# Row products of two token chunks with seven block products for eight, columns first, sums by DMA

## The chip, the cores and the metric

The kernel runs on one core of a Trainium2 chip. The metric is device time in microseconds of one launch, taken as the median of several runs. A core has five engines with instruction queues of their own: PE (TensorE, matmuls; PEld is its weight load), DVE (VectorE), ACT (ScalarE), POOL (GpSimd) and SP, which here only issues DMA transfers. They meet through semaphores.

## The reference

The input is attention data q, k, v of 2 batches, 8 heads, 768 positions, head size 64, and five weight matrices. Three steps follow one another:

- block attention: every query sees the keys closer than 16 positions and 24 block summaries (maximum of 32 keys, mean of 32 values), with a softmax over both;
- layer 1 on the 1536 tokens x 512: `g = x @ w_gate`, `val = x @ w_val`, then `(silu(g) * val) @ w_out`, with 1536 hidden columns;
- layer 2: `h = x @ w_in` with 2048 hidden columns, a piecewise square (0 below -1, h above 1, `(h + 1)^2 / 4` between), then `@ w_out` to the 1536 x 512 result.

All arrays are fp32.

## The kernel before

**Tiling.** The 1536 tokens are three chunks of 512 (`CH`). Every fp32 matmul operand is cut in two parts, `hi` (rounded to fp32r) and `lo` (the rest), and one product is three matmuls: hi*hi, hi*lo, lo*hi (`PASSES`, `mm3` L985, matmul at L987). Hi comes from a copy on ACT or DVE (`copy` L383), lo from a subtraction (`subtract` L924, instruction at L926), nearly always on DVE. A product with a layer's first weights is called a column product, one with its `w_out` a row product.

**Chunk 0** is done first, beside the attention of all chunks (`step_jobs`, `use_jobs` L1096). Its weights are decoded there, kept in DRAM (`keep_pack` L911) and read again later.

**Chunks 1 and 2 are done jointly** (`JOINT`, in the trace from about 266 us). Their column products already use a scheme with seven block products in the place of eight (`FORMS`, `form` L1306, `quad_jobs` L1325): two halves of the inner dimension, two blocks of hidden columns and the two chunks make a 2 x 2 by 2 x 2 block product. It needs sums of weight blocks (`add_group` L1208, cut in `group_hi`, `group_lo`), sums of input blocks (`add_term` L1269, cut in `term_hi`, `term_lo`), and joins of the results (`fork` L1318, `join` L1322). Layer 1 has 12 such quads, layer 2 has 8; each is seven forms of six matmuls of 512 columns.

Their row products are plain. `row_jobs` (L1374) issues, per chunk and per 128 hidden columns f, four row products of 128 outputs or 128 tokens (`row_product` L1005) into four accumulators in PSUM; `row_feed` (L1364) reads the kept weights and cuts them once per chunk, and `split_hidden` (L1171) cuts each hidden tile once. The rows of chunk 1 stand between the columns; those of chunk 2 follow. Each layer ends with copies out of PSUM (`y_out` L1405, or `put_jobs` L1085 with a store).

**Order.** Every piece of work is a job with its engines and durations, a rank, what it needs and which buffers it takes. `Plan.emit` (L127) is a list scheduler: it picks again and again the ready job with the least modelled start plus `URGE * rank`, chooses the engine that ends first by the modelled cost, and emits it. So it fixes the order of instructions on each engine's queue, SP's too; at run time each engine takes its queue in that order and waits for semaphores. The ranks are built from the constants `T`.

Of the kernel before, what the change touches and what calls it, by code (L numbers as in the profile page):

```python
# [25 lines left out]
 'urge': 0.00016,  # L26
 'weight': (0.925, 772.894, 0.282, 0.289),
# [3 lines left out]
 'd': (-5637.212, 41085.045),  # L31
 'load': (3008.479, 4747.053),
 'high': (-2836.042, 3239.532),
 'bits': (-935.349, 1886.602),
 'keep': (-57947.518, -5594.531),
 'read': -11449.662,
 'hi': (-27701.488, 1102.421),
 'lo': (-11590.763, -2406.109),
 'head_rank': (5076.154, -7290.563, -60395.485, -15458.656),
 'half_rank': -29616.131,  # L40
 'start': 464.292,
 'unit': 1.932,
 'e0': 462.563,
 'a1': (62.363, 14.301),
 'a2': (116.213, 16.636),
 'x': (617.322, 3982.825),
 'j': (2797.217, 10463.422),
 'g': (1.248, 6.748),
 'q': (0.007, 0.113),
 'jr': (1234.441, 846.231),  # L50
 'jw': (1404.409, 766.537),
 'rw': 858.964,
 'js': (-6034.078, 1900.145),
 'gh': (746.555, 1544.378),
 'gl': -1712.874,
 't': 484.136,
 'th': 822.2,
 'tl': -35.6,
 'qp': (-30.096, -19.417, -3.899, 35.81, 32.684, -24.767, -40.513),
 'qf': -562.767,  # L60
 'qj': -1653.995,
 'qa': 2416.954,
 'rs': 3036.454,
 'rh': 887.986,
 'x2': 255.064,
 'r2': (400.241, 30033.282),
 'first': (-5645.576, -144.845),
 'st_q': (-2034.21, 345.71),
 'st_qt': (-732.561, -1914.119),
 'st_sc': (-685.966, -444.589),  # L70
 'st_mx': (-35663.85, -1356.97),
 'st_ex': (-3778.03, 3307.182),
 'st_iv': (-5276.379, 81.698),
 'st_no': (742.266, -11947.766),
 'st_wt': (-4363.695, 165.258),
 'st_pt': (-52297.254, -1058.814),
 'st_av': (-394.819, -213.378),
 'st_xh': (133.16, 1680.548),
 'st_xl': (-10069.461, -3131.586),
 'kl': (-42181.744, 4874.082),  # L80
 'kp': (3666.397, -5596.737),
 'kt': (-3814.781, -1844.408),
 'km': (-77721.471, 514.179),
 'kc': (2433.202, -51674.2),
 'vl': (-198.108, 134.248),
 'vm': (2794.065, -1853.404),
 'vs': 26403.355,
 'vo': (-29543.71, -26442.98),
 've': (-15678.039, 5229.978),
 'ql': (-31980.946, -7672.979),  # L90
# [141 lines left out]
def tile_block_attention_ffn(  # L232
# [1141 lines left out]
    def row_jobs(c, st, fs, t):  # L1374
# [6 lines left out]
        for f in fs:  # L1381
            row_feed(c, st, f, t + UNIT * (f - fs[0]))
# [107 lines left out]
```

## Time and profile before

| what | value |
|---|---|
| runs | 613.59, 615.02, 615.07 us; median 615.02 us |
| span of the profiled execution | 612.5 us |
| PE / DVE / ACT / POOL busy | 98% / 82% / 57% / 4% |
| matmuls | 3737 |
| moved by DMA | 95.01 MB |

The profile gives the span of its execution, from the first instruction to the last, and no time of its own for what lies around it; the span is 2.5 us below the median. A busy PE is not a PE at its peak, since matmuls are pipelined; the chain of waits and the spacing of matmuls tell its pace. A line number is often that of a helper: L987 is every matmul with cut operands, L385 a copy on ACT, L389 a copy on DVE, L926 a subtraction; the names of output and inputs tell them apart (`acc_y` are row products; `qg`, `qv`, `qi` are column products of chunks 1 and 2; `pg`, `pv`, `pi` those of chunk 0).

### The profile page before, as it was taken

How to read it: one execution, taken by the hardware profiler on the slowest of the kernel's cores; microseconds unless marked ns; L12 is line 12 of the kernel's file. 1: busy time of each engine (PE TensorE's matmuls, PEld its weight loads, DVE VectorE, ACT ScalarE, POOL GpSimd, SP SyncE). 2: the span in 40 equal slices, each digit the busy share in tenths (PEclk: the TensorE clock that was granted, in tenths of full speed). 3: DMA queues.
4: the chain of work that ended last, by engine and by line, in shares of the span. 5: the costliest groups of instructions: out<-in, count | busy, mean ns of one | idle time of the engine just before them, and what ended most of it. 6: DMA issues, size and time to landing. Idle time of an engine off the chain costs nothing.

```text
span 612.5 us, 9841 instructions
## 1 busy us (share of the span) xinstructions
PE 600.7 (98%) x3737; PEld 498.4 (81%) x3737; DVE 502.4 (82%) x910; ACT 347.4 (57%) x634; POOL 26.8 (4%) x54
## 2 busy tenths in 40 slices
PE   8699999999999999999999999999999999999997
PEld 7589888778888888888888888888888888888886
DVE  4788999989899898887788877788888897886662
ACT  5787687877979576454443433322268554742112
POOL 3320201000000000000000000000000000000000
PEclk9979999999999999999999999999999999999999
DMA  8999996999896398132110211123300131103411
GB/s 228 291 303 279 328 303 251 327 266 317 315 339 206 138 307 309 71 139 68 70 68 1 103 70 68 35 104 102 138 20 16 34 138 35 36 0 116 160 35 69
DMA packets 79199, 95.01 MB, mean 155 GB/s; under 512 B 36272, under 2 KB 62128, under 8 KB 79152
## 3 DMA queue, kind: packets, MB, share of 16 engines
q1 hardware_dynamic: 79152, 94.39, 47.9%
q8 instruction: 29, 0.48, 0.3%
q14 instruction: 18, 0.15, 0.1%
HBM read 73.40 MB, written 20.97 MB: 154 GB/s over the span
## 4 chain that ended last, share of the span: by engine, by line
PE 96%; DMA 1%; SPq 1%; ACT 1%; POOL 0%; issue 0%; ACTq 0%; POOLq 0%
PE acc_y L987 38%; PE qi L987 12%; PE qv L987 9%; PE qg L987 9%; PE pi L987 7%; PE pv L987 6%; PE pg L987 6%; PE px L588 2%; PE sc L637 2%; PE pt L683 1%; DMA raw<-in_moe_w_val_dram 1%; PE pk L518 1%; SPq L442 1%; PE pq L569 1%; PE pk L296 1%; SPq L884 1%
## 5 line engine op out<-in xcount | busy, mean ns | idle before, releaser
L987 PE MATMUL acc_y<-dd,h 128*128 128x512 f32 (+1 forms) x387 | 88.4, 387 | 0.0
L987 PEld LDWEIGHTS acc_y<-dd,h 128*128 128x128 f32 x387 | 72.4, 188 | 14.9
L987 PE MATMUL acc_y<-h,dd 128*128 128x512 f32 x288 | 66.1, 389 | 0.0
L987 PEld LDWEIGHTS acc_y<-h,dd 128*128 128x128 f32 x288 | 54.1, 188 | 11.2
L385 ACT ACTIVATE dd<-wf 128x1024 fp32r<-128x1024 f32 x25 | 26.4, 1057 | 61.3 <-PE acc_y L987 61.3
L987 PE MATMUL qi<-xj,wjs 128*128 128x512 f32 x192 | 46.4, 389 | 0.0
L987 PE MATMUL acc_y<-wA,h 128*128 128x512 f32 x192 | 45.8, 389 | 0.0
L903 DVE SCALAR_TENSOR_TENSOR wb<-dd 128x1024 int32<-128x1024 int32 x34 | 41.6, 1227 | 2.3 <-ACT dd L385 1.4
L926 DVE TENSOR_TENSOR wA<-wb,wA 128x1024 fp32r<-128x1024 f32 x34 | 41.6, 1231 | 1.8 <-ACT wA L385 1.1
L987 PE MATMUL pi<-y,wA 128*128 128x512 f32 x128 | 42.4, 392 | 0.0
L987 PEld LDWEIGHTS qi<-xj,wjs 128*128 128x128 f32 x192 | 36.0, 188 | 7.5
L987 PEld LDWEIGHTS acc_y<-wA,h 128*128 128x128 f32 x192 | 36.0, 188 | 7.5
L894 ACT ACTIVATE dd<-raw 128x1024 f32<-128x1024 f32 x34 | 38.8, 1144 | 1.4 <-DMA raw<-in_moe_w_val_dram 1.3
L987 PE MATMUL acc_y<-h,wA 128*128 128x512 f32 x144 | 36.5, 399 | 0.0
L987 PE MATMUL qg<-xj,wjs 128*128 128x512 f32 x144 | 36.4, 389 | 0.0
L987 PE MATMUL qv<-xj,wjs 128*128 128x512 f32 x144 | 36.2, 389 | 0.0
L987 PE MATMUL pg<-x,wA 128*128 128x512 f32 (+1 forms) x112 | 35.2, 371 | 0.0
L987 PE MATMUL qi<-xj,wjo 128*128 128x512 f32 x144 | 34.9, 389 | 0.0
L926 DVE TENSOR_TENSOR dd<-wf,dd 128x1024 fp32r<-128x1024 f32 x28 | 34.2, 1224 | 0.3 <-ACT dd L385 0.2
L987 PE MATMUL pv<-x,wA 128*128 128x512 f32 (+1 forms) x112 | 34.3, 369 | 0.0
L926 DVE TENSOR_TENSOR h<-r,h 128x512 fp32r<-128x512 f32 x47 | 32.4, 692 | 2.1 <-ACT h L385 0.7
L385 ACT ACTIVATE dd<-raw 128x1024 int32<-128x1024 uint32 x28 | 31.9, 1140 | 0.0
(163 smaller groups left out, 1198.8 us busy)
## 6 DMA issues: line engine op xcount, KB each, us to landing
raw<-in_moe_w_out_dram SPq DMA_DIRECT2D x14, 1024.0 KB, 6.3
raw<-in_moe_w_in_dram SPq DMA_DIRECT2D x16, 512.0 KB, 7.3
wf<-kept_z SPq DMA_DIRECT2D x16, 512.0 KB, 3.2
raw<-in_moe_w_gate_dram SPq DMA_DIRECT2D x12, 512.0 KB, 7.1
raw<-in_moe_w_val_dram SPq DMA_DIRECT2D x12, 512.0 KB, 7.6
kept_g<-wb SPq DMA_DIRECT2D x12, 512.0 KB, 5.6
wj<-kept_g SPq DMA_DIRECT2D x12, 512.0 KB, 4.3
wf<-kept_o SPq DMA_DIRECT2D x12, 512.0 KB, 3.2
```

The source lines that it names most:

```text
L296: nc.tensor.transpose(t[:, 0:P], ident, ident)
L385: nc.scalar.activation(out, in_, AF.Copy, scale=scale)
L442: nc.sync.dma_start(out=vwin[0:KW, w], in_=bass.AP(src.tensor, src.offset, [[D, KW], [S * D, H], [1, D]]),)
L518: nc.tensor.matmul(cols[h * D:(h + 1) * D, r], kraw[b, p][one, h, r], ident[one, one], start=True, stop=True, skip_group_check=True)
L569: nc.tensor.transpose(pq[:, r * P:(r + 1) * P], raw[:, r].rearrange("p h d -> p (h d)"), ident)
L588: nc.tensor.matmul(px[h * D:(h + 1) * D, col:col + QT], vwin[0:KN, w, 2 * p + h], pT[0:KN, 2 * h + w // 2, w % 2 * QT:(w % 2 + 1) * QT], s ...
L637: nc.tensor.matmul(scs[h][j * QT:(j + 1) * QT, w // 2], qT[head, (w + j) * QT:(w + j + 1) * QT], kwin[p][head, s * WPS + w + j], start=Tru ...
L683: nc.tensor.transpose(pt[0:KN, w * P:(w + 1) * P], v_["sm"][:, w], ident)
L894: nc.scalar.activation(x[:, 0], raws[k][:, :, :, 1].bitcast(F32), AF.Prelu, scale=2.0 ** -112, alpha=2.0 ** 32)
L903: nc.vector.scalar_tensor_tensor(b, x[:, 0], 3, x[:, 1], op0=ALU.logical_shift_left, op1=ALU.bitwise_or)
L926: e.tensor_tensor(out, a, b, op=ALU.subtract)
L987: nc.tensor.matmul(dst, lhs(a), rhs(b), start=first and i == 0, stop=last and i == 2, **more)
```

## The change

- **Rows of chunks 1 and 2.** `row_jobs` and `row_feed` go. `stage_rows` pairs the hidden tiles (2j, 2j+1), takes the two chunks as the other block dimension and the two halves of the 512 outputs as the third, and does seven products per pair, in the order 1, 2, 5, 3, 6, 7, 4 over all pairs. `row_form` issues them: in layer 1 two groups of three matmuls with 512 columns, in layer 2 four groups of three matmuls with 256 columns. Hidden tiles are added in place (`add_side`), cut once per product and pair (`cut_side`: hi on ACT, lo on DVE) into one of 14 cells, the buffers that the input terms of the columns have had before. Weights are cut once per product and half of the pairs (`cut_weight`).
- **Order of a layer.** All its columns come first, then its rows, so every hidden tile of a layer is held; `MORE` adds 14 buffers. The seven forms of a quad come in the order 1, 5, (4 of the quad before), 6, 2, 3, 7.
- **Sums by DMA.** Sums of weight blocks, of input blocks and of hidden tiles are done in place, by a DMA issued on POOL's queue that adds to its destination (`SWD`), or by a DVE addition; the planner chooses by its modelled end. The sums of the row weights go by such a DMA only and are kept in DRAM (`sum_jobs`).
- **Silu.** For the chunks 1 and 2, one ACT instruction (`swish`) takes the place of Tanh on ACT and a DVE instruction.
- **Ranks.** `settle` works back through the needs of the joint part and ranks each job by its latest due time. All constants in `T` are new, those of chunk 0 and of the attention too. All eight PSUM banks serve the joint part (`QB`).

The core of the diff:

```diff
+    def settle(self, names, base, scale, lead):
+        due, users, state = {}, {}, {}
+        for name in names:
+            for x in self.jobs[name][3]:
+                users.setdefault(x, []).append(name)
+        waiting = {n: len(users.get(n, ())) for n in names}
+        ready = [n for n in names if not waiting[n]]
+        while ready:
+            name = ready.pop()
+            engines, rank, fn, needs, *rest = self.jobs[name]
+            kind, us = next(iter(engines.items()))
+            if kind in ("DMA", "SWD"):
+                us = 2.0 + us[0] + us[1]
+            due[name] = min([rank] + [due[x] - 0.3 - us for x in users.get(name, ())])
+            at = base + scale * (due[name] - lead.get(name[0], 0.0))
...
+                    if engine == "SWD":
+                        size = jobs[name][0]["SWD"][1]
+                        cost = max(start + us + self.DMA_START, free.get("moved", 0.0)) + size
+                        cost += self.WEIGHT["SWD"]
...
+    MORE = [f"e{i}" for i in range(14)]
+    JS = tuple(SLOTS + ["kord"] + MORE)
+    CELLS = tuple(f"c{i}" for i in range(14))
...
+    def swish(h, src, ring):
+        u = us[h] = slot(ring, "u")
+        nc.scalar.activation(u, src(), AF.Silu)
...
+    def read_sums(st, i):
+        t = sums[st, i] = wp.tile(
+            [P, 2, 4, 256], F32, tag="raw", name="sj", bufs=plan.rings["raw"])
+        for s, (j, z) in enumerate(((0, 0), (1, 0), (1, 0), (1, 1))):
+            part = slice(256 * z, 256 * z + 256)
+            if st == 1:
+                nc.sync.dma_start(out=t[:, :, s], in_=kept["g", 2 * i + j][:, :, part])
+                continue
+            for e in range(2):
+                nc.sync.dma_start(out=t[:, e, s], in_=kept["i", 4 * i + 2 * e][:, j, part])
...
     def add_group(st, i, s, engine):
-        w = plain[st, i]
-        if s == 0:
-            sums[st, i] = wp.tile(
-                [P, 2, 4, 256], F32, tag="raw", name="sj", bufs=plan.rings["raw"])
-        both = [w[:, :, x] if x < 4 else sums[st, i][:, :, x - 4] for x in SUMS[s][:2]]
-        nc.vector.tensor_tensor(
-            sums[st, i][:, :, s], *both, op=SUMS[s][2])
+        x = SUMS[s]
+        t = sums[st, i][:, :, s]
+        y = plain[st, i][:, :, x] if x < 4 else sums[st, i][:, :, x - 4]
+        if engine == "SWD":
+            nc.gpsimd.dma_start(out=t, in_=y, accum_op=ALU.add)
+        else:
+            nc.vector.tensor_tensor(t, t, y, op=ALU.add)
...
+    def add_term(st, k, b, engine):
+        x, (c, z) = operand(st, k, b), TERMS[b]
+        y = flat[st, c, k + HALF * z]
+        if engine == "SWD":
+            nc.gpsimd.dma_start(out=x, in_=y, accum_op=ALU.add)
+        else:
+            nc.vector.tensor_tensor(x, x, y, op=ALU.add)
...
+    RP = (1, 2, 5, 3, 6, 7, 4)
+    PLAIN = {1: (0, 0), 2: (1, 0), 4: (1, 1)}
...
+    def add_weight(st, g, key, other):
+        src = wsrc[st, g, other] if isinstance(other, str) else kept_part(st, g, *other)
+        nc.gpsimd.dma_start(out=wsrc[st, g, key], in_=src, accum_op=ALU.add)
...
+    def cut_weight(st, g, p, sign, what, engine, *ring):
+        n = PAIRS[st] // 2
+        if ring:
+            wcut[st, g, p] = wp.tile(
+                [P, 2, 4, 256], F32R, tag="wA", name="wr", bufs=plan.rings["wA"])[:, :, 0:n]
+        parts(engine, wcut[st, g, p], wsrc[st, g, p], sign, what)
...
+    def add_side(st, j, a, b, engine):
+        x, y = us[side(st, j, a)], us[side(st, j, b)]
+        if engine == "SWD":
+            nc.gpsimd.dma_start(out=x, in_=y, accum_op=ALU.add)
+        else:
+            nc.vector.tensor_tensor(x, x, y, op=ALU.add)
+
+    def cut_side(st, j, p, what, engine, *ring):
+        if ring:
+            bcut[st, j, p] = cell(ring[0])
+        parts(engine, bcut[st, j, p], us[side(st, j, SIDE[p])], 1.0, what)
+
+    def row_form(st, j, p, us_, *rings):
+        for ring in rings:
+            sides[st, us_[0][0], {1: "a", 2: "d", 5: "c"}[p]] = bank(ring, "r" + "oz"[st - 1])
+        n = PAIRS[st] // 2
+        w, b = wcut[st, j // n, p][:, :, j % n], bcut[st, j, p]
+        first, last = j == 0 and p in (1, 2, 5), j == PAIRS[st] - 1
+        for u, t in us_:
+            dst = sides[st, u, {2: "d", 5: "c", 3: "c"}.get(p, "a")]
+            if st == 1:
+                mm3(dst, lambda a: w[:, a, u * P:(u + 1) * P], lambda x: b[:, x], first, last,
+                    skip_group_check=p not in (1, 2, 5))
+            else:
+                m = 2 * u + t
+                mm3(dst[:, 256 * t:256 * t + 256], lambda a: b[:, a, m * P:(m + 1) * P],
+                    lambda x: w[:, x], first and not t, last, skip_group_check=True)
...
+    PAIRS = {1: F1 // 2, 2: F2 // 2}
+
+    def stage_rows(st, t):
+        n, half = PAIRS[st], PAIRS[st] // 2
+        us_pe = 6 * MM if st == 1 else 12 * 0.12
...
+                job(("rl", *n_), {"DMA": (0.4, 1.4, 1)}, LATE,
+                    lambda _, ring, a=n_: read_weight(*a, ring),
...
+                job(("wl", *n_), {"DVE+": cut[2]}, LATE,
+                    lambda e, a=n_, sign=sign: cut_weight(*a, sign, "lo", e), [("wh", *n_)], (),
+                    [(("rl", *n_), 0)])
...
+        seq = [(p, j) for p in (1, 2) for j in range(n - 1)] + [(1, n - 1), (2, n - 1)]
+        seq += [(p, j) for p in RP[2:] for j in range(n)]
+        S = lambda j, which: side(st, j, which)
+        for j in range(n):
+            made = lambda *w, j=j: [("u3", *S(j, x)) for x in w]
+            adds = {
+                5: ("B11", "B12", made("B11", "B12") + [("bl", st, j, 1)], []),
+                6: ("B11", "B22", made("B22") + [("bl", st, j, 5)], [(("u", *S(j, "B22")), 0)]),
+                7: ("B12", "B22", made("B22") + [("bt", st, j, 5)], [(("u", *S(j, "B22")), 0)]),
+                4: ("B21", "B11", [("bl", st, j, 2), ("bt", st, j, 6)], [(("u", *S(j, "B11")), 0)]),
+            }
+            for p, (a, b, needs, gives) in adds.items():
+                job(("bt", st, j, p), {"SWD": (1.2, 1.7), "DVE+": 0.7}, LATE,
+                    lambda e, j=j, a=a, b=b: add_side(st, j, a, b, e), needs, (), gives)
...
+        for x, (p, j) in enumerate(seq):
+            needs = [("bt", st, j, p)] if p in (5, 6, 7, 4) else [("u3", *S(j, SIDE[p]))]
+            job(("bh", st, j, p), {"ACT": 0.64}, LATE,
+                lambda e, ring, j=j, p=p: cut_side(st, j, p, "hi", e, ring), needs, (CELLS,),
+                follows=prior("bh", ("bh", st, j, p)))
+            job(("bl", st, j, p), {"DVE+": 0.7}, LATE,
+                lambda e, j=j, p=p: cut_side(st, j, p, "lo", e), [("bh", st, j, p)], (),
+                [(("u", *S(j, end_of[p])), 0)] if p in end_of else [])
...
+            for p, name, src in ((1, "s1", "a"), (5, "c5", "c"), (6, "u2", "a")):
+                job(("rf", st, u, name), {"ACT": 0.61, "DVE": 0.7}, at(p, n - 1) + fr,
+                    lambda e, ring, u=u, name=name, src=src: side_copy(st, u, name, src, e, ring),
+                    list(dict.fromkeys(done[p, u])), (JS,))
+            for p, name, src, how, c, z, gives in (
+                    (2, "s1", "d", "-+"[st - 1], C1, 0, [(first[2, u], 0)]),
+                    (3, "u2", "c", "r", C2, 0, [(first[5, u], 0)]),
+                    (7, "c5", "a", "r-"[st - 1], C2, 1, [])):
...
+        steps = ((5, "n22", (0, 1), [("sn", *m, "n22")]), (6, "n22", "n11", [("rk", *m, 5), ("sn", *m, "n11")]),
+                 (3, "n22", (1, 0), [("rk", *m, 6)]), (7, "n11", (0, 1), [("ra", *m, 6)]))
+        for p, key, other, needs in steps:
+            job(("ra", *m, p), {"SWD": (1.2, 3.4)}, LATE,
+                lambda e, key=key, other=other: add_weight(st, g, key, other), needs)
+            job(("rk", *m, p), {"DMA": (0.4, 1.4, 1)}, LATE,
+                lambda *_, p=p, key=key: keep_sum(st, g, p, key), [("ra", *m, p)], (),
...
+    QB = BANKS + ACCS
...
+        line = [x for x in order if x[0] == st]
+        turns = []
+        for x, one in enumerate(line):
+            turns += [(one, 1), (one, 5)] + ([(line[x - 1], 4)] if x else [])
+            turns += [(one, p) for p in (6, 2, 3, 7)]
+        turns.append((line[-1], 4))
+        at = {turn: t + 6 * MM * x for x, turn in enumerate(turns)}
         for i in range(GROUPS[st]):
-            group_jobs(st, i, t0 + step * i + T["jw"][st - 1])
+            group_jobs(st, i)
             for e in range(2):
-                quad_jobs((st, i, e), t0 + step * i + half * e, JS)
-        n = (F1, F2)[st - 1]
-        each = 2 * step / (2 if st == 1 else 4)
-        for f in range(n):
-            row_jobs(C1, st, [f], t0 + each * (f // 2 + 1) + T["jr"][st - 1] + UNIT * (f % 2))
-        t0 += each * n / 2 + T["jr"][st - 1] + T["r2"][st - 1]
-        for f in range(n - END):
-            row_jobs(C2, st, [f], t0 + UNIT * f)
-        row_jobs(C2, st, [*range(n - END, n)], t0 + UNIT * (n - END))
+                quad_jobs((st, i, e), {p: at[(st, i, e), p] for p in FORMS}, JS)
+        t += 6 * MM * len(turns)
+        stage_rows(st, t)
+        for g in range(2):
+            sum_jobs(st, g)
+        t += 7 * PAIRS[st] * (6 * MM if st == 1 else 12 * 0.12)
```

## Rows read from the trace of the kernel before

**Rows 1.** The page: the span, and the first part (busy time by engine).

```profile
span 612.5 us, 9841 instructions
...
PE 600.7 (98%) x3737; PEld 498.4 (81%) x3737; DVE 502.4 (82%) x910; ACT 347.4 (57%) x634; POOL 26.8 (4%) x54
```

**Rows 2.** The page: the chain that ended last, by engine and by line.

```profile
PE 96%; DMA 1%; SPq 1%; ACT 1%; POOL 0%; issue 0%; ACTq 0%; POOLq 0%
PE acc_y L987 38%; PE qi L987 12%; PE qv L987 9%; PE qg L987 9%; PE pi L987 7%; PE pv L987 6%; PE pg L987 6%; PE px L588 2%; PE sc L637 2%; PE pt L683 1%; DMA raw<-in_moe_w_val_dram 1%; PE pk L518 1%; SPq L442 1%; PE pq L569 1%; PE pk L296 1%; SPq L884 1%
```

**Rows 3.** Windows: busy us (instructions) of PE, PEld, DVE, ACT, POOL; clock; DMA share; GB/s.

```profile
0.00:40.00 40.00, 32.03 (x583) 27.73 (x584) 24.95 (x103) 26.68 (x69) 11.88 (x41) 0.91 1.01 268
40.00:266.00 226.00, 226.00 (x1643) 186.90 (x1642) 205.73 (x417) 170.78 (x345) 11.07 (x10) 1.00 0.82 264
266.00:445.40 179.40, 179.40 (x793) 148.59 (x792) 147.30 (x213) 70.93 (x104) 2.59 (x2) 1.00 0.23 81
445.40:609.30 163.90, 163.25 (x724) 135.14 (x722) 124.45 (x183) 78.90 (x118) 1.29 (x1) 1.00 0.17 60
```

**Rows 4.** The chain in order of time at the two seams: start, us, what.

```profile
257.71 8.16 PE acc_y L987 x36
265.87 1.36 PE qg L987 x6
...
435.87 9.55 PE acc_y L987 x42
```

**Rows 5.** Groups by line and form, TensorE's row products: busy us, mean ns.

```profile
L987 PE MATMUL acc_y<-dd,h 128*128 128x512 f32 x381 | 87.7, 389 | 0.0
L987 PE MATMUL acc_y<-h,dd 128*128 128x512 f32 x288 | 66.1, 389 | 0.0
...
L987 PE MATMUL acc_y<-dd,h 128*128 128x256 f32 x6 | 0.9, 282 | 0.0
```

**Rows 6.** The chain: 256-column and 512-column matmuls; then the group of weight loads.

```profile
48.60 2.15 PE pv L987 x18
...
195.15 2.72 PE pi L987 x12
...
L987 PEld LDWEIGHTS pv<-x,wA 128*128 128x128 f32 x112 | 20.3, 189 | 3.6 <-issue 0.6
```

**Rows 7.** Groups by line and form, VectorE.

```profile
L926 DVE TENSOR_TENSOR h<-r,h 128x512 fp32r<-128x512 f32 x47 | 32.4, 692 | 2.1 <-ACT h L385 0.7
L926 DVE TENSOR_TENSOR wjs<-sj,wjs 128x1024 fp32r<-128x1024 f32 x20 | 24.4, 1221 | 0.1
...
L926 DVE TENSOR_TENSOR wjo<-wj,wjo 128x768 fp32r<-128x768 f32 x20 | 19.1, 955 | 0.3
L389 DVE CAST h<-r 128x512 fp32r<-128x512 f32 x41 | 17.5, 426 | 17.4 <-PE acc_y L987 16.5
...
L1214 DVE TENSOR_TENSOR sj<-wj 128x512 f32<-128x512 f32 x20 | 13.2, 687 | 1.5 <-DMA wj<-kept_g 1.4
```

**Rows 8.** Groups by line and form, ScalarE.

```profile
L385 ACT ACTIVATE wjs<-sj 128x1024 fp32r<-128x1024 f32 x17 | 17.9, 1055 | 8.4 <-PE qv L987 7.4 <-PE qg L987 1.0
...
L385 ACT ACTIVATE qu<-qi 128x512 f32<-128x512 f32 x16 | 9.6, 599 | 13.4 <-PE qi L987 13.2
...
L385 ACT ACTIVATE wjo<-wj 128x768 fp32r<-128x768 f32 x9 | 7.5, 837 | 1.6 <-PE qv L987 1.1 <-PE acc_y L987 0.4
...
L385 ACT ACTIVATE h<-u 128x512 fp32r<-128x512 f32 x8 | 5.1, 634 | 4.2 <-PE acc_y L987 4.0 <-DVE u L1040 0.3
...
L385 ACT ACT_TABLE_LOAD x1 | 1.3, 1283 | 0.8 <-PEq L1472 0.8
```

**Rows 9.** DMA queue (packets, MB, share); issues with KB each and us to landing.

```profile
q1 hardware_dynamic: 79152, 94.39, 47.9%
...
out_dram<-o SPq DMA_DIRECT2D x11, 256.0 KB, 2.5
...
qraw<-in_q_dram SPq DMA_DIRECT2D x4, 256.0 KB, 6.9
```

**Rows 10.** Windows: the stretch in which TensorE waited most.

```profile
20.00:40.00 20.00, 14.20 (x238) 12.02 (x238) 14.05 (x48) 14.71 (x36) 3.31 (x4) 0.83 1.04 312
```

More of the change, by code (lines that the diff above doesn't have):

```diff
@@ L114 @@
     SWITCH, LEAD, TILED = 0.11, 0.09, ("sc", "av", "kp", "vm")
-    WEIGHT = dict(zip(("ACT", "DVE", "DVE+", "POOL"), T["weight"]))
+    WEIGHT = dict(zip(("ACT", "DVE", "DVE+", "POOL", "SWD"), (*T["weight"], T["swd"])))
     def __init__(self, rings):
@@ L125, in job @@
             engines, rank, fn, tuple(needs), takes, tuple(gives), after, tuple(follows))
+    def settle(self, names, base, scale, lead):
[13 more added lines that the diff above has]
+            at = base + scale * (due[name] - lead.get(name[0], 0.0))
+            self.jobs[name] = (engines, at, fn, needs, *rest)
+            for x in needs:
+                if x in waiting:
+                    waiting[x] -= 1
+                    if not waiting[x]:
+                        ready.append(x)
+        assert len(due) == len(names)
     def emit(self):
@@ L209, in emit @@
                 free["DMA"], end[name] = at, landed[-1]
+            elif engine == "SWD":
+                at = start + us + self.DMA_START
+                free["moved"] = max(at, free.get("moved", 0.0)) + jobs[name][0]["SWD"][1]
+                end[name] = free["moved"] + self.DMA_END
             elif engine == "PE":
@@ new lines, in tile_block_attention_ffn, with cell, parts @@
+    holders = {}
+    def cell(ring):
+        k, i = divmod(int(ring[1:]), 7)
+        if k not in holders:
+            holders[k] = big.tile([P, 7, 2, CH], F32R, tag=f"big{k}", name=f"cells{k}")
+        return holders[k][:, i]
+    def parts(engine, t, src, sign, what):
+        if what == "hi":
+            copy(engine, t[:, 0], src, sign)
+        elif sign == 1.0:
+            subtract(engine, t[:, 1], src, t[:, 0].bitcast(F32))
+        else:
+            nc.vector.scalar_tensor_tensor(
+                t[:, 1], src, sign, t[:, 0].bitcast(F32), op0=ALU.mult, op1=ALU.subtract)
@@ L1297, in term_jobs @@
[L1297 to L1302 removed]
+                made[c, z] = ("f", st, c, k + HALF * z) if st == 1 else results[c, k + HALF * z][0]
@@ new lines, in term_jobs @@
+                gives[c, z] = ((made[c, z] if st == 1 else results[c, k + HALF * z][1]), 0)
+        split = lambda b: ("tl", st, k, b)
+        term = lambda b: ("t", st, k, b)
+        needs = {3: [split(0), made[C2, 0]], 5: [term(3), made[C2, 1]],
+                 4: [split(2), term(3), term(5)], 6: [split(1), term(4)]}
+        done = {4: [gives[C1, 0]], 6: [gives[C2, 1]]}
+        for b in (3, 5, 4, 6):
+            job(term(b), {"SWD": (1.2, 1.7), "DVE+": 0.7}, LATE,
+                lambda e, b=b: add_term(st, k, b, e), needs[b] + (before if st == 1 else []), (),
+                done.get(b, ()))
```

498 lines of the change are left out of this document (303 added, 195 removed).

## The prediction

> **What bounds the kernel now.** I began with the page's first part: PE is busy 98% of the span, DVE 82%, ACT 57% [rows 1]. A busy share says little for an engine that pipelines, so the chain that ended last came next: 96% of it is PE, and 38% is the row products `acc_y` alone [rows 2]. The windows then show where: in the first 40 us PE is busy 32.0 us and the granted clock is 0.91; from 40 us on it never idles until its last matmul [rows 3]. The chain in order of time has no seam either: the joint part begins at 265.87 us with the first `qg` matmul directly behind chunk 0, and layer 2 starts where the 9.55 us of `acc_y` end, at 445.4 us [rows 4]. So from 40 us on the kernel lasts as long as its matmuls need to be issued. A matmul removed there shortens the run by its spacing, as long as the other engines still deliver in time. The spacing is not the mean duration of 389 ns [rows 5], which holds the latency: 12 matmuls of 512 columns take 2.72 us, 0.2267 each, and 18 matmuls of 256 columns take 2.15 us, 0.1194 each [rows 6].
>
> The window shows the margin of the others: DVE 147.3 of 179.4 us in layer 1 and 124.5 of 163.9 in layer 2, ACT 70.9 and 78.9, DMA share 0.23 and 0.17 [rows 3].
>
> **The matmuls.** Before, layer 1 has 2 chunks x 12 hidden tiles x 4 x 3 = 288 row matmuls of 512 columns and layer 2 has 2 x 16 x 4 x 3 = 384. The trace agrees: 381 and 288 of 512 columns with 6 of 256 are 672 [rows 5], and 672 x 0.2267 = 152.3 us.
>
> After, layer 1 needs 7 products x 6 pairs x 6 = 252 of 512 columns: 57.1 us for 65.3, **8.2 us less**. Layer 2 needs 7 x 8 x 12 = 672 of 256 columns: 672 x 0.1194 = 80.2 us for 87.1, **6.8 us less**; the narrower form takes back 4.1 of the 10.9 us that seven for eight would give. Column products stay 840. Sum on PE: **15.0 us less**.
>
> The narrow form loads new weights for each matmul, and one load is busy 189 ns [rows 6], more than 119. But the 18 matmuls at 0.1194 also had one load each, so loads overlap, and I count nothing more.
>
> **VectorE and ScalarE in the rows.** What was one cut per hidden tile and chunk becomes one per product and pair. Layer 1's rows (57.1 us on PE): 42 lo cuts x 0.692, 14 weight cuts of 768 elements x 0.955, 6 joins x 0.687, 14 input cuts for layer 2 x 0.692 give 29.1 + 13.4 + 4.1 + 9.7 = 56.3 us on DVE, durations from [rows 7]. That is 98% of the stage before a single addition; the 24 additions of hidden tiles and 8 of input blocks would be 32 x 0.687 = 22.0 us more. ACT has 42 hi cuts x 0.634, 14 x 0.837, 8 copies x 0.599 and 14 x 0.634 there: 26.6 + 11.7 + 4.8 + 8.9 = 52.0 us, from [rows 8]. Layer 2's rows (80.2 us): DVE 56 x 0.692 + 14 x 1.221 + 6 x 0.687 = 60.0 us, additions 32 x 0.687 = 22.0; ACT 56 x 0.634 + 14 x 1.055 + about 5 = 55 us.
>
> So this is the place to watch: layer 1's rows fit only if additions leave DVE or work slides out of the stage. Both are open to it: the columns of layer 1 (114.3 us on PE) hold on DVE 12 x (0.955 + 1.221) + 36 x 0.687 + 24 x 0.687 = 67.3 us, so the first lo and weight cuts can be made there as cells come free, and the last input cuts may lie behind the first forms of layer 2. Silu on ACT takes 24 x 0.687 = 16.5 us of DVE away, already left out of the 67.3. Layer 2's columns (76.2 us) hold 8 x (0.955 + 1.221) + 24 x 0.687 + 32 x 0.687 = 55.9 us. I take 0 for exposure. Bounds: 0, and 56.3 + 22.0 - 57.1 - 8 = 13 us with all additions on DVE and 8 us slid out (6 + 6 cuts at 0.692); I stay at 0, because DVE was at 82% of layer 1's window before, its work too came in lumps, and PE showed no wait [rows 3].
>
> **Additions by DMA.** The trace has no transfer from POOL's queue, only the hardware queue [rows 9], so their price is bounded from both sides: 2.5 us to landing for 256 KB to `out`, 6.9 us for 256 KB of q in the crowded start [rows 9]; as the DMA share is 0.2, I take about 3. What covers them: a hidden tile is summed once its last cut is made and read two products later, 2 x 8.16 = 16.3 us in layer 1 and 22.9 in layer 2, less 1.3 us of cuts. Nothing is exposed at 2.5 or at 6.9. The queue's pace matters more: if all 24 go by POOL, they must pass within six products, 49 us, or 2.0 us each; 32 within 69 us, 2.1 each. At half the additions the limit is 4.1 us. POOL itself is nearly free in these stretches, 2.6 and 1.3 us [rows 3]. What waits behind a late one: POOL's next addition, then ACT's hi cut, in whose in-order queue the cuts and copies of other products stand, then DVE's lo cut, then PE. The 16 weight sums stand in the same queue but are due a whole column stage later; each result is kept by an SP transfer that waits for it, and SP's next reads of column weights stand behind that. One such wait of 6.9 us lies within the 19 us that a column group lasts. Counted at 0.
>
> **Seams.** Between the layers the last product, 4, gives only the block C1,1. Layer 2 starts with forms 1, 5, 6, which do not read it: 3 x 1.36 = 4.1 us of cover for a copy, a hi and a lo cut, 0.60 + 0.63 + 0.69 = 1.9 us plus handoffs, less than 3. At the first seam the joins of the last quad are needed 13.6 us later. Counted at 0; if the queues of ACT and DVE are late, this is where it shows first. A second function table for Silu costs one load of 1.28 us [rows 8], maybe two, on ACT that has room beside the columns: 0. The end of the kernel keeps its form, a copy of 256 columns and a store.
>
> **The first 266 us** have the same work in another order. There only the first 40 us have air, 8.0 us of idle PE [rows 3], and I see no reason for either sign: 0, with -3 and +3 as bounds.
>
> **Sum.** 612.5 - 15.0 = 597.5 us of span; with the 2.5 us to the median, **600.0 us**. 0.3% (1.8 us) is about what a measurement of this kernel can tell from no change, so faster means under 613.2.
>
> **Rivals.**
>
> *DVE becomes the bound in layer 1's rows.* For it: the 98% above, and a static order in which one late cut holds all behind it. Against it: the additions can leave. It gives back 3 to 13 us: 603 to 613, likeliest 607. Chance 0.18.
>
> *POOL's queue is late (slower).* It decides in the row stages from 2.0 us per addition when all go there, 4.1 us at half. At half and 5 us each: 12 x 5 - 49 = 11 us in layer 1, 16 x 5 - 69 = 11 in layer 2, so 622. PE's waits there can also cost clock: in 20 to 40 us, with PE busy 14.2 of 20, the grant fell to 0.83 [rows 10], which lies on the way from 2.4 to 1.2 GHz. For it: nothing in the trace shows such a transfer's pace. Against it: free engines and a planner that keeps an addition on DVE when its model sees DVE free. Chance 0.12. DVE's copies stand beside it: one 128x512 cast takes 0.426 us [rows 7], and if each addition on POOL lost one such stretch, 2.0 us of pace would leave 1.6 for the addition itself; 0.04 of the 0.12 is for that. The Trainium skill (SBUF — State Buffer, "Who interferes with whom") states such a hold: a DVE copy in a two-port mode locks GpSimd out while it writes descriptors. By that rule an addition would wait behind casts, not behind subtractions; no run here shows it yet.
>
> *The new order loses in the first 266 us.* Every constant is new, and PE's waits there were 8.0 us; with 5 to 15 us lost the result is 605 to 615. Chance 0.06.
>
> That the change removes fewer matmuls than counted is excluded by the diff: the count follows from its loops.
>
> **Numbers.** The forecast, all of the 15 us kept but 3, has 0.64 and lies from 596 to 604. The first rival stretches to 613, the third to 615, the second lies beyond. 596 to 610 leaves out the 0.12, some 0.05 of the others above, and 0.03 below. Faster: 0.64 + 0.16 + 0.03 = 0.83; same 0.05; slower 0.12.
>
> **What would show it.** Right: some 3986 matmuls (3737 - 675 + 252 + 672), with 672 of 256 columns in layer 2's rows; their spacing 0.119 us; windows from 40 us on with PE full; the joint part 328 us instead of 343. Wrong: PE idle ended by DVE or ACT cuts in layer 1's rows (first rival), by a DMA issued on POOL, or ACT's cuts waiting for one (second), a clock under 1.00 after 40 us, or a joint part that starts later than 269 us (third).

## The result, and the profile after

The changed kernel takes **600.73 us** (median of 4 runs, 599.51 to 601.72) against 615.05 us of the kernel before in the same session (4 runs, 613.59 to 615.22): a ratio of 0.9773, interval [0.9753, 0.9792]. The forecast was 600.0. The profiled execution of the changed kernel is its fastest of the four (599.51).

The page of the changed kernel, its span, its busy times and the engines of the chain that ended last; they answer to [rows 1] and [rows 2]:

```profile
span 597.2 us, 10769 instructions
...
PE 587.8 (98%) x3984; PEld 500.2 (84%) x3984; DVE 494.0 (83%) x901; ACT 405.7 (68%) x746; POOL 77.6 (13%) x105
...
PE 96%; ACT 1%; DMA 1%; SPq 1%; issue 0%; DVE 0%; POOL 0%; POOLq 0%
```

TensorE is still the bound: 98% and 96%, as before. The other engines carry more (ACT 57% to 68%, POOL 4% to 13%) inside a shorter span, and none of them appears in the chain with more than 1%. The row products, by form (busy us, mean ns, idle time before), answer to [rows 5]:

```profile
L1017 PE MATMUL rz<-wr,cells 128*128 128x256 f32 x672 | 81.6, 283 | 0.6 <-ACT ra L408 0.5
...
L1017 PE MATMUL ro<-cells,wr 128*128 128x512 f32 x252 | 58.1, 390 | 0.0
```

These are the 252 and 672 of the forecast. Their spacing and the place of the seams stand in the chain in order of time (start us, us, what), which answers to [rows 4] and [rows 6]:

```profile
255.89 8.16 PE acc_y L1017 x36
264.05 6.80 PE qg L1017 x30
...
427.57 1.36 PE qi L1017 x6
428.93 8.16 PE ro L1017 x36
437.09 72.08 PE qi L1017 x318
...
516.97 70.57 PE rz L1017 x588
587.56 0.39 ACT ra L408
...
592.61 0.39 ACT ra L408
...
593.05 0.63 PE rz L1017 x3
```

588 matmuls of 256 columns in 70.57 us are 0.1200 us each. Both seams are tight: the joint part starts 0 us behind chunk 0's last `acc_y`, and one form of layer 2 (`qi`, 1.36 us) stands ahead of layer 1's last product. Only at the very end does TensorE wait twice, for a ScalarE copy; three matmuls stand behind the second. The windows (columns as in [rows 3]), from 40 us on by the parts ahead of and in the joint part, then of one of its stages, layer 1's columns:

```profile
40.00:264.05 224.05, 223.67 (x1617) 183.70 (x1616) 197.67 (x405) 167.42 (x336) 10.48 (x9) 1.00 0.90 275
264.05:592.60 328.55, 328.40 (x1761) 285.00 (x1760) 268.35 (x389) 209.26 (x333) 56.76 (x59) 1.00 0.73 189
```

```profile
264.05:375.57 111.52, 111.52 (x493) 92.35 (x493) 87.60 (x125) 54.30 (x85) 11.07 (x10) 1.00 0.70 198
```

To the end of TensorE's last matmul (593.68 us) the joint part lasts 329.63 us. Before it lasted from 265.87 to 608.66 us, 342.79 us, as the last piece of TensorE in the chain of the kernel before shows:

```profile
544.70 63.96 PE acc_y L987 x285
```

That is **13.16 us** of the 15.3 us by which the two profiled spans differ. The rest is two smaller pieces: the part ahead of it ends 1.8 us earlier (264.05 for 265.87), and the tail behind the last matmul is 0.3 us shorter (3.52 for 3.84). The granted clock is 1.00 in the joint part, and TensorE is full there up to the two waits at the end.

The DMA part of the page shows a new queue: packets, MB and share of GpSimd's queue, then two issues of it with us to landing. Before there was no such queue and no such transfer [rows 9].

```profile
q0 software_dynamic: 14112, 20.45, 20.6%
...
r<-r POOLq DMA_DIRECT2D x16, 256.0 KB, 8.0
u<-u POOLq DMA_DIRECT2D x14, 256.0 KB, 8.4
```

The planner put 40 of the 56 additions of hidden tiles on GpSimd (15 of 24 in layer 1, 25 of 32 in layer 2) and 16 on VectorE. The share of the DMA engines in the joint part rose from 0.20 to 0.73.

### The profile page after: what moved, and what is told of

Its sections match the earlier page's. It is cut to its first block, busy times and chain, and to the rows that moved or that the text cites. A ratio compares the mean times of both kernels' runs of the same rounds, so it can differ in the third digit from the quotient of the medians.

```text
span 597.2 us, 10769 instructions
## 1 busy us (share of the span) xinstructions
PE 587.8 (98%) x3984; PEld 500.2 (84%) x3984; DVE 494.0 (83%) x901; ACT 405.7 (68%) x746; POOL 77.6 (13%) x105
## 4 chain that ended last, share of the span: by engine, by line
PE 96%; ACT 1%; DMA 1%; SPq 1%; issue 0%; DVE 0%; POOL 0%; POOLq 0%
PE rz L1017 14%; PE acc_y L1017 13%; PE qi L1017 13%; PE ro L1017 10%; PE qv L1017 10%; PE qg L1017 10%; PE pi L1017 8%; PE pg L1017 5%; PE pv L1017 5%; PE px L611 2%; PE sc L660 2%; PE pt L706 1%; PE pk L541 1%; DMA vrest<-in_v_dram 1%; PE pq L592 1%; PE pk L315 1%
## 5 line engine op out<-in xcount | busy, mean ns | idle before, releaser
L1017 PE MATMUL rz<-wr,cells 128*128 128x256 f32 x672 | 81.6, 283 | 0.6 <-ACT ra L408 0.5
L1017 PEld LDWEIGHTS rz<-wr,cells 128*128 128x128 f32 x672 | 81.1, 192 | 1.2 <-ACT ra L408 1.0
L1017 PE MATMUL ro<-cells,wr 128*128 128x512 f32 x252 | 58.1, 390 | 0.0
L1017 PEld LDWEIGHTS ro<-cells,wr 128*128 128x128 f32 x252 | 47.2, 188 | 10.2 <-ACT ru L408 0.4
L1017 PE MATMUL qi<-cells,wjs 128*128 128x512 f32 x192 | 46.8, 389 | 0.0
L1017 PEld LDWEIGHTS qi<-cells,wjs 128*128 128x128 f32 x192 | 36.0, 188 | 7.4
L1017 PE MATMUL qi<-cells,wjo 128*128 128x512 f32 x144 | 36.1, 389 | 0.0
L1017 PE MATMUL qv<-cells,wjs 128*128 128x512 f32 x144 | 35.6, 389 | 0.0
L1017 PE MATMUL qg<-cells,wjs 128*128 128x512 f32 x144 | 35.6, 389 | 0.0
L1017 PEld LDWEIGHTS qv<-cells,wjs 128*128 128x128 f32 x144 | 27.0, 188 | 5.6
```

The source lines that it names most:

```text
L1017: nc.tensor.matmul(dst, lhs(a), rhs(b), start=first and i == 0, stop=last and i == 2, **more)
```

## Experiments

All ratios are to the kernel before. The kernel after has 0.9773 [0.9753, 0.9792].

**What seven products are worth by themselves.** Two runs keep the columns-first order and put eight plain products back, in both layers and in layer 2 alone (the block sums and additions go with them).

```diff
-        stage_rows(st, t)
-        for g in range(2):
-            sum_jobs(st, g)
-        t += 7 * PAIRS[st] * ...
+        (stage_rows8 if st in EIGHT else stage_rows)(st, t)
+        if st not in EIGHT:
+            for g in range(2):
+                sum_jobs(st, g)
+        t += (8 if st in EIGHT else 7) * PAIRS[st] * ...
```

`stage_rows8` is `stage_rows` with products 1 to 8, each of one block of the input and one of the weights, added up in PSUM in pairs. In the first run EIGHT is (1, 2):

> Columns first as in the changed kernel, but both layers' rows by eight plain block products, in the same matmul forms; no sums of hidden tiles or of row weights, weights and hidden tiles cut once per product. PE has 288 in place of 252 matmuls of 512 columns and 768 in place of 672 of 256: 8.2 + 96 x 0.1194 = 11.5 us more. DVE has 8 x 6 x 0.692 + 16 x 0.955 + 9.7 = 58 of 65.3 us in layer 1's rows. Cover theory: 600.7 + 19.7 = 620.4 us, within 3. Rival, the order of columns and rows or the sums cost the change something that this saves: under 615 us. Rival, the seven products bring little and the new first part or the order brings the gain: 605 us or less.

Measured: 619.09 us, 1.0091 [1.0071, 1.0112]. In the second it is (2,):

> As the run before, in layer 2 alone; layer 1 as changed. PE has 96 matmuls of 256 columns more, 11.5 us. Cover theory: 600.7 + 11.5 = 612.2 us, within 2; with the run before, layer 1 alone is the rest, 8.2 us. Rivals as there: under 609, or 603 and less.

Measured: 612.12 us, 0.9966 [0.9954, 0.9978]. The group of layer 2's row products in the first of the two, and the last matmuls of the chain in the first and in the second:

```profile
L1017 PE MATMUL rz<-wr,cells 128*128 128x256 f32 x768 | 93.2, 283 | 0.6 <-ACT ra L408 0.6
```

```profile
613.27 0.63 PE rz L1017 x3
...
605.77 0.64 PE rz L1017 x3
```

So without the saved product the new kernel is *slower* than the old by about 5 us (619.09 for 614.18 us of the kernel before in that session): 768 matmuls at 0.1200 are 92.2 us where 384 at 0.2267 were 87.1. What the saved products bring is read from the traces, because the medians of the kernel after and of these two come from different sessions. From the start of the joint part (264.52 and 264.82 us here) to the last matmul it takes 349.38 and 341.59 us, and 329.63 in the kernel after. The saved products bring 19.75 us, 11.96 of them in layer 2 and 7.79 in layer 1; counted, they are 96 x 0.1200 + 36 x 0.2267 = 11.5 + 8.2. The order of columns first gives no gain of its own here. That its part is to make room is argued: no run has the seven products in the old order.

**Who must do the additions.** The additions that GpSimd's transfers do are done by VectorE, at the same places of the order (also those of the column sums and input blocks; the 16 sums of row weights stay).

```diff
-            nc.gpsimd.dma_start(out=x, in_=y, accum_op=ALU.add)
+            nc.vector.tensor_tensor(x, x, y, op=ALU.add)
```

> The 50 additions that the changed kernel issues as DMA on POOL (40 of hidden tiles, 6 of column weight blocks, 4 of input blocks) are executed by DVE at the same place of the order; the 16 weight sums stay on POOL. Cover theory (the saving is PE's spacing, the rest is hidden with room): DVE gets 15 more additions of 0.686 us in layer 1's rows, where it is busy 50.2 of 55.4 us, so 60.5 us no longer fit and PE waits some 3 to 8 us there; layer 2's rows go to 60.9 + 25 x 0.686 = 78 of 83.4 us and hold; result 603 to 609 us. Rival, sums by DMA bring nothing: 600.7 within 1.8 us. Rival, DVE sets the pace of the whole joint part: over 613 us.

Measured: 613.81 us, 0.9994 [0.9977, 1.0011]: the whole gain is gone. Three windows, of layer 1's rows, of layer 2's and of a stretch of layer 2's, with the longest wait of TensorE in the rows (line waited for: us, times, longest):

```profile
384.00:443.30 59.30, 55.67 (x239) 43.86 (x238) 59.27 (x92) 40.53 (x66) 3.49 (x3) 1.00 0.30 76
...
515.40:607.40 92.00, 86.15 (x681) 84.62 (x680) 74.91 (x113) 52.30 (x85) 0.00 (x0) 0.96 0.20 75
...
535.00:582.00 47.00, 41.29 (x341) 40.68 (x339) 47.00 (x72) 30.76 (x50) 0.00 (x0) 0.98 0.04 12
```

```profile
PE rz L1017 <- ACT ru L408: 5.0, 1, 5.0
```

VectorE is busy 59.27 of 59.30 us: this is the first rival, in its place. Layer 1 takes 178.3 us in place of 173.0, layer 2 164.1 in place of 155.5 (to TensorE's last wait). The expectation was too low, because it had layer 2's rows hold. By their total they do (74.91 of 92.00 us), but the work bunches: from 535 to 582 us VectorE is busy all the time, and the long wait, for a ScalarE copy that stands behind cuts waiting for VectorE, lies at that stretch's end. Behind it the granted clock is 0.50, which is 1.2 GHz, for 4 us. Might an order planned for this have saved it? The same additions with only VectorE offered to the planner:

```diff
-                job(("bt", st, j, p), {"SWD": (1.2, 1.7), "DVE+": 0.7}, LATE,
+                job(("bt", st, j, p), {"DVE+": 0.7}, LATE,
```

(and so for the input blocks and column sums.)

> As the run before, but the planner knows that only DVE does these additions, and orders anew. Cover theory: the total of DVE work in layer 1's rows is the same, but cuts and additions can slide into the columns, which hold DVE busy 92.3 of 117.6 us; PE waits 0 to 5 us, result 601 to 606 us, and less than the run before. Rival, sums by DMA carry the gain: over 609 us. Rival, they bring nothing: 600.7 within 1.8 us in both runs.

Measured: 614.79 us, 0.9996 [0.9971, 1.0022]. It doesn't: TensorE now waits for VectorE's cuts in the rows of both layers.

```profile
PE ro L1017 <- DVE cells L956: 2.9, 2, 1.8
PE rz L1017 <- DVE cells L956: 1.4, 1, 1.4
```

In both orders, then, the transfers are what lets the gain come out.

**All on GpSimd.** The other way round: only the transfer is offered for the 56 hidden additions.

```diff
-                job(("bt", st, j, p), {"SWD": (1.2, 1.7), "DVE+": 0.7}, LATE,
+                job(("bt", st, j, p), {"SWD": (1.2, 1.7)}, LATE,
```

> All 56 additions of hidden tiles go by DMA on POOL, 16 more than before, order planned anew. Cover theory: at 1.1 to 1.2 us each 24 need 29 of 49 us and 32 need 38 of 69 us, and a landing of 8 us lies within the 15 us of two products; 600.7 within 1.8 us. Rival, POOL's queue is near its limit: PE waits that end with DMAs of POOL, and 603 us or more.

Measured: 609.07 us, 0.9909 [0.9879, 0.9938], some 8 us worse than the kernel after. TensorE's waits in the joint part (besides the 0.5 us at the end that the kernel after has too), the stretch up to the first of them and the one behind the second, and the landings of the largest group:

```profile
PE ro L1017 <- ACT more L408: 2.2, 1, 2.2
PE ro L1017 <- ACT ru L408: 1.9, 1, 1.9
PE rz L1017 <- ACT rc L408: 1.6, 1, 1.6
```

```profile
379.98:407.30 27.32, 25.14 (x111) 20.23 (x110) 25.22 (x38) 18.63 (x31) 13.55 (x17) 1.00 1.09 250
...
425.85:445.42 19.57, 19.57 (x79) 16.07 (x80) 16.16 (x25) 12.71 (x21) 3.52 (x3) 0.91 0.55 135
```

```profile
u<-u POOLq DMA_DIRECT2D x21, 256.0 KB, 11.8
```

The waits alone are 5.7 us of the 8. More is in the clock column: after the second wait the granted clock is 0.91 over 19.57 us, which costs 0.09 x 19.57 = 1.8 us more with TensorE full. Together that is 7.5 us. But what makes the result copies (`more`, `ru`, `rc`) late? In the first of the two stretches GpSimd is idle half of the time and the DMA share is 1.09, so the transfers were the first suspect. The same order with a plain copy in place of the accumulation (its output lacks these additions):

```diff
-            nc.gpsimd.dma_start(out=x, in_=y, accum_op=ALU.add)
+            nc.gpsimd.dma_start(out=x, in_=y)
```

> The order of the run with all 56 hidden additions on POOL, word for word, but each is a plain copy where that run accumulates, so the additions of hidden tiles are left out and the output differs. That run took 609.07 us, its additions landed 12 us after issue and the DMA engines' share stood at 1.08 to 1.12 where they bunch. Theory A, an accumulating transfer holds the DMA engines about twice as long per byte and they are what runs out: the share falls by a third there, landings to under 6 us, PE's waits go, result 600 to 603 us. Theory B, POOL's pace of about 1 us per issue or its in-order waits run out: landings and result stay, 607 to 610 us.

Measured: 608.67 us, 0.9913 [0.9898, 0.9928]. The landings of the same group (the other large one, `r<-r`, fell from 12.6 to 4.3 us):

```profile
u<-u POOLq DMA_DIRECT2D x21, 256.0 KB, 4.5
```

Transfers that land in little over a third of the time change nothing: layer 1's two waits end at the same copies after the same matmuls, and are as long, though the DMA share from 380 to 445 us falls from 0.90 to 0.63. So neither landing nor DMA load made the waits of *this* order. Is it GpSimd's pace? Its records of single issues are longer with the addition (0.86 us and more, for 0.54), but they overlap. Here are two neighbours in the run with the additions; they start 0.54 us apart, and those with plain copies (404.10 and 404.63) 0.53:

```profile
403.93 0.86 POOL L1484 DMA_DIRECT2D more<-u  x1 [4.81 <-DVE cells L956]
404.47 3.85 POOL L1484 DMA_DIRECT2D u<-u  x4
```

To try the pace itself, the kernel after was run with a small extra transfer (8 KB) ahead of each of its 40 hidden additions:

```diff
+            spare = dram.tile([P, 16], F32, name=f"spare{st}_{j}_{a}{b}")
+            nc.gpsimd.dma_start(out=spare, in_=ident[:, 0:16])
             nc.gpsimd.dma_start(out=x, in_=y, accum_op=ALU.add)
```

> The changed kernel in its own order, with one more DMA of 128 x 64 bytes to a spare place in DRAM issued on POOL ahead of each of the 40 hidden additions there, which doubles what POOL's queue passes and adds 0.3 MB of traffic. Theory A, the DMA engines' time is what is scarce: 600.7 us, at most 603. Theory B, POOL's pace is: about 15 additions in layer 1's rows and 24 in layer 2's each come 1 us later in a row, and the result is 606 us or more.

Measured: 601.47 us, 0.9786 [0.9765, 0.9806]; TensorE's only wait in the joint part is the 0.5 us at the end. Its layer 1 rows:

```profile
385.00:441.00 56.00, 55.99 (x248) 46.03 (x247) 50.77 (x77) 41.71 (x68) 23.15 (x30) 1.00 0.81 175
```

GpSimd's queue has room for twice the issues; in this kernel the second rival's pace falls. That leaves the in-order queues. In the order with all on GpSimd, ScalarE's copy `more` stands behind seven cuts of hidden tiles and a weight cut, and these began only when TensorE freed a cell (402.2). From the chain:

```profile
402.81 2.37 ACT cells L408 x5
...
406.76 0.49 ACT more L408
```

So I moved these copies to VectorE at the same places:

```diff
-        copy(engine, t, sides[st, u, src], ...)
+        copy("DVE", t, sides[st, u, src], ...)
```

> The order of the run with all 56 hidden additions on GpSimd, word for word on TensorE, with one edit: the copies of finished row products out of their banks (twelve, eight in the rows of layer 1 and of layer 2 that the order put on ScalarE among them) are all done by VectorE at the same places. In that run TensorE waits 5.7 us in three stretches, each ended by such a copy on ScalarE, and VectorE is busy 49.4 of 65 us around the first two. Theory (ScalarE works its queue in order, and these copies stand behind five or more cuts of hidden tiles, which wait for late additions): the three waits for ScalarE's copies are gone or below 1 us together, the joint part falls from 336.7 to 331 +-1.5, time 603.5 us (602.5 to 605). Rival (the copies are late in whatever queue, since the cuts' second halves stand in VectorE's queue in the same order behind the same additions): the waits stay, now ended by VectorE's copies, and the time is 608 to 610.

Measured: 610.91 us, 0.9947 [0.9928, 0.9966]. TensorE's two longest waits in the rows:

```profile
PE ro L1017 <- ACT cells L408: 3.1, 1, 3.1
PE ro L1017 <- DVE ru L412: 2.0, 2, 1.6
```

The theory falls, as put: the waits didn't go, they moved, one to VectorE's copies and one to ScalarE's cuts. Both queues are late in that order, and relieving one loads the other. Last, the sixteen additions that the kernel after has on VectorE are made transfers too, in the kernel after's own order, so that order and additions come apart:

```diff
 # in add_side, the branch of the additions planned for VectorE
-            nc.vector.tensor_tensor(x, x, y, op=ALU.add)
+            nc.gpsimd.dma_start(out=x, in_=y, accum_op=ALU.add)
```

> The kernel after, its order word for word, with one edit: the 16 hidden additions that VectorE does (9 in layer 1, 7 in layer 2, 0.69 us each) are accumulating transfers of GpSimd at the same places, so that all 56 are, as in the run with all additions on GpSimd that was ordered anew and took 609.07 us. TensorE's order is unchanged. Theory A (what that run lost is in the order that was written for it, not in the additions' being transfers): time 601 to 603, no wait of TensorE over 1 us in the rows of either layer. Theory B (the 16 on VectorE are the ones needed soon: a sum that lands 8 to 12 us after its issue and not after 0.7 is late there, and with it the cuts behind it in ScalarE's and VectorE's queues, which work in order): waits of TensorE in the rows, ended by a cut or by a result copy, 5 to 15 us together, time 606 to 616; the waits lie right behind the former VectorE additions (379 to 402 us and 505 to 547 us).

Measured: 604.79 us, 0.9849 [0.9825, 0.9874], between the two theories. The chain in order of time around its one wait in the rows, and the windows from the wait's end to the end of layer 1 and of the 4 us behind the wait:

```profile
379.44 16.06 DMA sj<-sj
...
395.79 0.43 POOL sj L1262
...
396.51 0.21 POOL u L1484
...
397.07 8.90 DMA u<-u
...
406.05 0.06 ACT cells L408
...
406.58 0.59 ACT rc L408
...
407.21 18.15 PE ro L1017 x72
```

```profile
407.20:443.37 36.17, 36.15 (x151) 29.48 (x152) 28.14 (x42) 27.24 (x44) 10.39 (x11) 0.95 0.91 175
```

```profile
407.00:411.00 4.00, 3.79 (x10) 3.02 (x11) 0.96 (x1) 2.52 (x5) 1.82 (x3) 0.57 1.12 232
```

Here Theory B's mechanism stands in one chain: a transfer of a column sum takes 16.06 us to land (the two of that stage in the kernel after took at most 9.4), GpSimd's next ones wait behind it, a hidden tile's sum lands 8.90 us after that, ScalarE's cut waits for it, a result copy stands behind the cut, and TensorE waits 2.1 us. Then it runs its next 4 us at a granted clock of 0.57, between 1.2 and 2.4 GHz. Layer 1 is 177.0 us for 173.0: 2.1 of wait and 0.05 x 36.17 = 1.8 of clock. Layer 2 stays at 155.5, so the seven additions left to VectorE there are not needed, while the nine in layer 1 are worth 4 us. The 8 us of the run with all on GpSimd are another matter: its waits don't change with the landing, so they belong to the order written for it. Why the planner put its copies behind those cuts is open.

**Silu as one function.** A sigmoid on ScalarE and a product on VectorE in its place:

```diff
-        nc.scalar.activation(u, src(), AF.Silu)
+        nc.scalar.activation(u, src(), AF.Sigmoid)
...
+            job(("u2", *h), {dve: 0.7}, t + 0.7, lambda *_: gated(h, src), [gate], (), [held])
```

> For chunks 1 and 2 a sigmoid on ACT and a product by its input on DVE take the place of the one Silu instruction. 24 DVE instructions of 0.69 us, 16.5 us, come back in layer 1's columns, where DVE is busy 92.3 of 117.6 us. Cover theory: they fit, 600.7 within 1.8 us. Rival, DVE is the bound there: 605 to 617 us.

Measured: 602.16 us, 0.9799 [0.9769, 0.9828], not to be told from the kernel after. The window of layer 1's columns:

```profile
265.98:384.00 118.02, 118.02 (x522) 97.75 (x522) 106.02 (x155) 58.71 (x90) 12.49 (x11) 1.00 0.68 200
```

VectorE does 106.0 us of work in 118.0 us there, and TensorE is full all the same (its one new wait is 0.7 us, for a ScalarE copy in layer 2): the 16.5 us that Silu spares are hidden beside the columns either way.

**The part ahead, and the end.** The first run ranks everything ahead of the two layers with the constants of the kernel before:

```diff
-                    cost = start + self.WEIGHT.get(kind, 0.0) * us
+                    cost = start + (self.WEIGHT if name in self.joint else self.EARLY).get(kind, 0.0) * us
...
-        job(("load", k), {"DMA": load_us(k)}, t + T["load"][late(k)], ...
+        job(("load", k), {"DMA": load_us(k)}, t + OLD["load"][late(k)], ...
```

> The columns-first, seven-product work of the kernel after, but everything ahead of the two layers (the projections, the attention, chunk 0 and its layers) ranked with the constants, ring sizes and engine weights of the kernel before. In the kernel after that part ended at 264.05 us, in the one before at 265.87. Theory (the 1.8 us of the span that the columns, the products and the additions do not explain are the new ranks of the first part): the first part ends at about 265.9 again, the joint part stays at 328.5 +-0.7, and the time is 602.5 us (601.8 to 603.3). Rival 1 (those 1.8 us came from somewhere else, such as work of the joint part that is no longer pulled ahead of its place): first part ends at 264.0, time 600.7. Rival 2 (the new ranks of the first part are needed by what follows, since loads and cuts for layer 1 are started there): the joint part itself gets longer than 331 us, time over 605.

Measured: 601.73 us, 0.979 [0.9768, 0.9811]; the first part ends at 266.80, the joint part is 329.63 us to the last matmul again (595.80 + 0.63 - 266.80). It reads like the theory, but doesn't carry it: kernels whose order ahead of the joint part is the same as in the kernel after end it at 264.05, 265.00, 265.94, 266.39 and 268.32 in their profiles. The 1.8 us lie within that spread. The second run has the last copies wait for both halves of their bank:

```diff
-                    [last[4, (u, z)]], () if z else (JS,), [(first[1, u], 0)])
+                    [last[4, (u, 0)], last[4, (u, 1)]], () if z else (JS,), [(first[1, u], 0)])
```

> One edit to the kernel after: the last two results of layer 2 are copied out of their bank only when both halves of it are done, so that no copy of one half stands between the last products of the other half. The order of the instructions on every engine is the same; only what the copies wait for differs. Theory (the two idle stretches of TensorE near the end, 0.46 us together, are its waiting for the copy of the other half of the same bank): waits for the copies gone, TensorE ends about 0.46 us earlier; the last copy starts when the last product is done, as now, but it now has both halves' copies behind it, 0.38 us more; time 600.6 us, within 0.3 of the kernel after. Rival (the end is worth more than that, because the first half's result also leaves sooner): 600.0 or less, a version that beats both. Other rival (the first half's copy and transfer, which now lie beside the last products, come after them): 601.5 or more.

Measured: 600.07 us (597.61 to 602.80), 0.9761 [0.9735, 0.9787]. Its chain near the end:

```profile
589.88 4.57 PE rz L1017 x38
...
594.48 0.38 ACT ra L408
```

TensorE runs through, and its last matmul ends 328.51 us behind the joint part's start (594.45 - 265.94) in place of 329.63: the two waits cost TensorE 1.1 us. About half of that reaches the end of the span, 332.6 us behind the start (598.5 - 265.94) in place of 333.15 (597.2 - 264.05). By the medians the two can't be told apart.

## Why the prediction was right

**The matmuls.** 252 and 672 came out, 3984 in all for the 3986 counted, with the loads hidden as [rows 6] had it. Counted: 15.0 us less; measured in the joint part, to the last matmul: 13.2. Of the difference, 1.1 us are the two waits at the end, as the run without them shows (328.51 us, 14.3 less than before), and 672 x (0.1200 - 0.1194) = 0.4 us is the spacing of the narrow form. Of the 14.32 us by the medians this term is by far the largest part, and the eight-product runs show it directly: 19.75 us for 19.7 counted. That the forecast met the median within 0.7 us is in part luck: the 1.1 us lost at the end were not counted, and some 0.8 us of gain that neither the joint part nor the tail explains (14.32 - 13.16 - 0.32) make up for most of them.

**VectorE in layer 1's rows** was rightly the place to watch, and 0 was right for the kernel as planned, but two terms behind it were mis-sized. The first is the 67.3 us that the columns were to hold on VectorE: up to the first row product, at 375.57 us, it is busy 87.6 of 111.5 us. Groups of that stretch:

```profile
L1264 DVE TENSOR_TENSOR sj<-sj,wj 128x512 f32<-128x512 f32 x11 | 7.5, 685 | 0.0
L1264 DVE TENSOR_TENSOR sj<-sj 128x512 f32<-128x512 f32 x10 | 6.9, 687 | 0.1
...
L956 DVE TENSOR_TENSOR cells<-u,cells 128x512 fp32r<-128x512 f32 x4 | 2.7, 686 | 0.7 <-ACT cells L408 0.7
L956 DVE TENSOR_TENSOR wr<-wr 128x768 fp32r<-128x768 f32 x2 | 1.8, 952 | 0.0
```

The count left out the sums of column weights, 21 of which VectorE does itself (14.4 us), ten hi copies of 768 elements (5.5) and cuts of layer 1's own input (5.3). "8 us slid out" was near: six of the rows' cuts (4.5 us) are made there, and eight cuts of layer 2's input (5.4 us) come behind the rows. The second is the bound of 13 us with all additions on VectorE, which was made for layer 1 alone. With them, layer 1 lost 5.3 us, less than the bound, but layer 2 lost 8.6; the step had 60.0 + 22.0 us on VectorE against 80.2 on TensorE there and counted nothing for it. With the additions kept on VectorE the first rival costs all of the gain (613.81, and 614.79 planned anew), the upper end of its range and not 607.

**Additions by DMA.** The step that failed is "as the DMA share is 0.2, I take about 3". Landing takes 8.0 and 8.4 us, beyond the upper bound of 6.9 from a plain load [rows 9], and the share is 0.73 because the change itself brings the transfers. It did no harm, since the step had 16.3 and 22.9 us of cover; what it missed is that cover per tile doesn't help where several tiles queue: with all on GpSimd, in the kernel after's order, 4 us come through in layer 1. The pace (limit 2.0 us, or 4.1 at half) was right: issues that stand ready start 0.54 us apart, and twice as many cost nothing measurable. The second rival's copies of VectorE were put as a hold of GpSimd's issues. By the Trainium skill (SBUF — State Buffer, "Who interferes with whom") such copies lock GpSimd out as it writes descriptors. No run here shows that hold, and none tests it: in the trace of the kernel after and in that of the run with all on GpSimd no cast on VectorE overlaps the issue of a hidden addition.

**Seams, Silu, tail.** Both seams cost 0, as counted. Silu's function table costs one load more (1.28 us on ScalarE, hidden). "The end of the kernel keeps its form" was off by 1.1 us of TensorE: the halves of one bank are now finished apart, and a copy of the first holds up the matmuls into the second.

**The first 266 us**, counted at 0 within 3, is 1.8 us shorter in this profile, which is less than the profiles differ among themselves.

## What to carry to other kernels

Where TensorE is full, a product saved is worth its matmuls' spacing, and nothing else in the change needs to be fast: the rest has only to arrive in time, so count each other engine's work stage by stage, in *every* stage, and where it bunches within one, before asking whether a helper engine is needed. When it is, split the work by who needs it when: late sums on the slow path, soon-needed ones on the fast engine. And a stall of 2 us in a full stretch can cost about double, when the granted clock falls behind it.

## What the runs showed of the hardware

An accumulating transfer from GpSimd costs the DMA engines much more than a plain one of the same 256 KB. In the same order it lands after 11.8 and 12.6 us against 4.5 and 4.3, and GpSimd's queue holds 22.3% of the 16 DMA engines' span against 15.4% for the same 23.34 MB (16 x (607.4 x 0.223 - 608.9 x 0.154) / 56 = 11.9 engine-us more for each addition). Its issue is recorded as 856 to 1211 ns in the mean of a group against 539 to 544, but issues that stand ready start as close to one another in either run (0.54 and 0.53 us). The Trainium skill (DMA: Bandwidth & Descriptors, "Anatomy of one DMA — SWDGE (gpsimd) path") gives a fit of some 2.0 us plus bytes over 436 thousand per us, an estimate of 2.6 us for these; the transfers measured here, plain ones too, are far from it.

One wait of TensorE of about 2 us was enough for the granted clock to fall below 1.00 behind it (0.57 over 4 us), though not behind each: after the first wait of the run with all on GpSimd (2.2 us) it stayed at 1.00, and after the same wait in the same order with plain copies it was 0.57 from 407 to 411 us. After the wait of 5.0 us with the additions on VectorE it was 0.50, which is 1.2 GHz, over 4 us.
